# Capped attention feeding a two-layer MLP on one core: last key chunk in array quarters, row sums of a pair of head pairs in 112 columns, constants filled by GpSimd

## The chip, the cores and the metric

The kernel runs on one core of a Trainium2 chip. The number compared is the device time of the whole program in microseconds (us): the median of three runs of the kernel before was 580.81 us (580.37 to 581.53). The profile shown here is of one further execution, which took 580.01 us.

## The reference, cut to what matters

```python
# q, k, v: (4 batches, 12 heads, 448 tokens, 64); scale = 1/8; cap = 30
scores = scale * q @ k.T
scores = cap * tanh(scores / cap)
attn = exp(scores - max) / (sum(exp(scores - max)) + 1e-9)
x = (attn @ v)  -> heads side by side: (4 * 448, 768)
h = x @ w_in                                             # w_in: (768, 2048)
g = where(h >= 1, h, where(h <= -1, 0, (h + 1)**2 / 4))
out = g @ w_out                                          # w_out: (2048, 768)
```

## The kernel before, in words

**Names.** Two heads that share a batch make a head pair; there are 6 pairs in a batch and 24 in all, n = 0 to 23, and `d = n // 2` counts pairs of head pairs. S is 448 queries, P is 128, D is 64, HS is 224. The 448 keys are cut in chunks c = 0, 1, 2 of 128 keys and c = 3 of 64 keys. PSUM has eight banks: two tiles `s` of two banks each for scores, `f0` and `f1` for the MLP's products, one bank `av` for attention times values, one bank `t` for the row sums and for their reciprocals spread over partitions.

**Attention of one pair n** (`attention`). `split` cuts the loaded q and k into two fp16 parts. `qk` multiplies them in three products on 64x64 quarters of TensorE's array, four matmuls at a time. `expo` runs tanh and exp on ScalarE and writes fp32 tiles `e`. `av` multiplies values by `e`; the two heads of the pair use the left and the right 64 columns of the array, two matmuls at a time. For the last chunk, which has 64 keys, the two heads lie in the two halves of the partitions crosswise, and the values have blocks of zeros so that a full 128-row matmul picks the right half (`last_av`, 224 columns). Pairs 12 to 17 (`HALVED`) use fp16 parts of `e` and of the values, three products each, the others fp32.

**Row sums.** `add` adds chunks of `e` on VectorE as far as `direct(n)` says, and `norm` sums over partitions with matmuls of a matrix of ones, four at a time in 32 columns of the array each, 224 columns of data: for n < 6 three groups of four fp32 matmuls (the added chunks 0 and 1, then chunk 2, then chunk 3), for n = 6 to 11 two groups, from n = 12 on one. Both n of one d add into bank `t`. `divide` takes a reciprocal of (128, 224), cuts it in three bf16 parts stacked over rows (`low`), spreads it over partitions with two matmuls per n of 224 columns (`sel`), and scales the copy `xf` of the bank `av`.

**MLP.** fp16 parts again, three products of 448 columns (`across`, in `h_mm`, `o_mm`, `product`). A matmul of 128 columns of weights is issued either whole or as two of 64 columns side by side; `Plan.narrow` picks the second where the neighbours in TensorE's order are attention matmuls of that shape. Batches 2 and 3 are computed with seven products for eight, at the end.

**Order.** `ORDER` is a table that lists every step and its engine; the program is issued in exactly that order on each engine, and TensorE works in order. Where `either` gives several engines, the table picks one. The MLP's matmuls of batch 0 begin once the attention of batch 0 is divided; from then on they stand between the attention steps of later batches.

Of the kernel before, what the change touches and what calls it, by code (L numbers as in the profile page):

```python
# [14 lines left out]
BF16 = mybir.dt.bfloat16  # L15
# [11 lines left out]
VC = 2 * NCK + 2  # L27
# [48 lines left out]
HS = S // 2  # L76

# [9 lines left out]
    "c-mEW1E5^V^L15qb#-@a+qP}nwr$(CZQITw#%{P9+uV)0`DX5&m*4-JyqCGRQ8;z#bU%Pt5E}&IfPuJxpdcQEgZK~u2m}*ALWl^7ATcBXhDeYUEF^;{kQ`D#N(c{;!9gmB2B{$pq=gbt64F6gC<PTE"  # L87
    "Jw%5L5CbwoOvnTcp&XQk%uorcK^ABPS;1g7C=a!uHhhE@5EUvzbtnVbp)pw0kOL|}Rj30Fb3zr!1vQ`vgu|9l6T)Lts0(c&H?)EXm<$_0Gspu&p+2;OyzmKzK|bgRouEB5hkEcC+CYBz0-d1%%z<xE"
    "5L&|+7z@Lp5PXFgI2T61NGJ@+u^SYD@6ZE^!Z^r+9bhU<gi$aJy1;lS1}ShJOoHOj6S~86NQsMKJ}iJ<5EFaDWEc$--~gn?70?H!z!HdsePJc^gQai~X22R42!o(MbcF%15N5++m<5YqImE_Quof=D"
    "@30zvfpt&_2g5SB1ZglX4uOqu1kS*(Z~`_%DqIhTARZotvk(VoLIu1GCt(Y0f>ZDZ9D{4{7yJfo@Hm`?t*{NU;&#{p*>D5wgg+rW?t$yD7ygD`cmsC9Zn%oq@IDmAD{vd`z<Kx&>fudz0C(Xb+`t@I"  # L90
    "1dHMYcmh}9C7y$uI1O*XJ$QxBU?1GZJNO)O;v;wgFQFK|g8P^YZ{chB2Oi@Ctcd#|B0j;lPznFR;&>gO!ae*K-oYDqi0|PkR>ps^3RcAra2H?WTP%U~u>nTHcUTQ0;}3{}QL!O@#Iy)_1*733M2tk~"
    "kgzdE$F|rGN8n?Kk8dzNenN#A@ENwp1o#4*;8)Cu9Wfyuz>=5<8B1X!e2<aoGj_nzxCs+u8SI3;@eB6Bk=Pe=V;&rZ$tWs4$0WD}zhPedfur#QX2MgL6u)CW%#ZysIYptd7>#1kI7Es`nXv#8jlqIA"
    "0OL?~EQ>X;DK^7?7?*&e({wCOikN1gCZVO6fKpOTtc9^@CdQ)L7>~+fc{G%YX5lg{LCvuR&c@}KhFW4cT7myzXY7J=un*P2gj5$d<3QYkD=|C`!mgNzGEjVKg<CN#b;H5f9WAZGB-8_k;6Y4H8EG4~"
    "#_>1-58+VEM2GQLbhI6N;#^EhgJ~kp!(o_$($Nl_gumf0cp4{T7CM8&@htYG`M4Sv;6hx3e_%<Pg0*QX_M<;>5w69ZxDL<ZdhAb`X&3&EyKxR3!3~&|7UKZggNvyY4WW&A6o=9<8cxS>FAk(Zv=2+u"
    "T&hFqDI1lg<Cud+P(?bABWXX*qZ3$;%1~meOG{`JEu{!FpDIyRDo+=%GF`-Kw2UHBF3L%la5Rmfu{4gx(*&AGlV~zcp{X>D_Rs>VLM!Mb=BDYioEB0Zsz-|`FIAxWw3qTxb!tdWX(b(|%ead2(`s5n"
    "Yw0h{PU~nN{f+zS7g|pnXd`W+8PteoQUNMR2Wd0?O25$-Izor&D9xf{REW0HaoR?w)fGBG4d?`2rE9cK6{g#?otn`}x=z2-DLPGOXb0`2o79rdsI&A3{YmHOJYArRbca6CCAv&^=?3kh8dQX8QZ2ei"
    "x2QR_qV?(rZC0P@3pJq!bf0F^SBj$=(>L0p9#U)iPHm_K?NFfhsYmpfp3qa;png%mDpaKQtH0<!imQ~`skW-N#44UTr{b$k>KQ$!7xa>}I-p+BYdWj`p~R{v6(dnbS>;qX6<$S95mh7=Sw&G%)xY$H"
    "-coydN9R=sdQTlGq3T4PsS71i8`Um#NVTK?R1%d`T~NE}14UEORRWbvrBEr=HuX2fP%%|1m0JC&y3$vbMx|Bd_=noAs_<oXP^DApRS!C>x>0iVn_A4f18vij{!$rKMwLnJQJK{VbzOC*KU6IBx4NPB"
# [1340 lines left out]
```

## Time and profile before

| what | value |
|---|---|
| median of three runs | 580.81 us |
| the profiled execution | 580.01 us |
| its span (first to last instruction) | 578.1 us |
| TensorE busy | 568.7 us, 98% |
| VectorE busy | 517.8 us, 90% |
| ScalarE busy | 420.6 us, 73% |
| GpSimd busy | 1.3 us |

Busy is the time in which at least one instruction of an engine was under way. Matmuls overlap each other, so that a gap shorter than a matmul's own length does not show as idle time. The span leaves out 1.9 us at the program's ends.

### The profile page before, as it was taken

The page shows a single profiled execution, that of the slowest core. Times are in us where ns is not written, and L with a number is a line of the kernel's source. Part 1 is how long each engine was busy: PE and PEld are TensorE (multiplying, and loading weights), DVE is VectorE, ACT ScalarE, POOL GpSimd, SP SyncE. Part 2 cuts the span into 40 slices and gives each one's busy share as a digit, 9 for nine tenths or more (in the row PEclk, how much of TensorE's full clock was granted, in tenths as well). Part 3 has the DMA queues.
Part 4 walks back from the last instruction along what each step waited for, and adds up shares of the span by engine and source line. Part 5 has one row for each costly group of instructions (what it writes and reads, how often), then busy time and mean ns, then how long its engine had stood idle before and what let it go on. Part 6 is the DMA issues. An engine that isn't in the chain of part 4 may idle for free.

```text
span 578.1 us, 13988 instructions
## 1 busy us (share of the span) xinstructions
PE 568.7 (98%) x5685; PEld 319.1 (55%) x5685; DVE 517.8 (90%) x1017; ACT 420.6 (73%) x703; POOL 1.3 (0%) x6
## 2 busy tenths in 40 slices
PE   7999999999999999999999999999999999999997
PEld 3444554545454555556654545566666666666675
DVE  7999999999999999999998865899899999998712
ACT  6999998968558579989999897557877786541200
POOL 0000000000000000000000000000000000000000
PEclk9999999999999999999999999999999999999999
DMA  8879581767878412311789999994566656653202
GB/s 302 306 249 352 177 299 77 282 241 249 317 252 274 183 56 88 104 56 57 227 271 290 337 307 325 308 292 142 158 225 201 207 185 211 200 176 123 88 33 83
DMA packets 57000, 120.11 MB, mean 208 GB/s; under 512 B 4962, under 2 KB 35426, under 8 KB 55394
## 3 DMA queue, kind: packets, MB, share of 16 engines
q1 hardware_dynamic: 56784, 119.07, 61.1%
q8 instruction: 45, 0.74, 0.5%
q14 instruction: 25, 0.20, 0.1%
q10 hardware_dynamic: 146, 0.10, 0.1%
HBM read 91.42 MB, written 27.72 MB: 206 GB/s over the span
## 4 chain that ended last, share of the span: by engine, by line
PE 53%; DVE 4%; ACT 1%; issue 0%; DVEq 0%; ACTq 0%
PE f L268 24%; PE s L268 12%; PE av L268 7%; PE t L268 4%; PE av L483 2%; PE s L407 2%; PE av L388 1%; PE t L504 1%; DVE wr L611 1%; DVE g L545 0%; DVE z L425 0%; PE av L470 0%; DVE sums L452 0%; DVE sums L444 0%; PE s L403 0%
## 5 line engine op out<-in xcount | busy, mean ns | idle before, releaser
L268 PEld LDWEIGHTS <-w 128*64 128x64 f16 (+1 forms) x2997 | 206.8, 107 | 145.7 <-issue 5.3
L268 PE MATMUL f<-x,w 128*64 128x448 f16 (+1 forms) x939 | 122.8, 353 | 0.4 <-DVE wr L611 0.3
L268 PE MATMUL f<-g,w 128*128 128x448 f16 (+1 forms) x774 | 121.7, 353 | 0.0
L415 ACT ACTIVATE e<-s,tsc 128x896 f32<-128x896 f32 (+1 forms) x96 | 84.9, 910 | 16.6 <-PE s L407 9.4
L416 ACT ACTIVATE e<-e,capb 128x896 f32<-128x896 f32 (+1 forms) x96 | 89.6, 948 | 0.5
L407 PE MATMUL s<-spl 64*64 64x448 f16 x864 | 51.3, 357 | 2.2 <-ACT e L415 1.8
L483 PE MATMUL av<-e,vt 128*64 128x448 f32 x216 | 45.6, 549 | 0.2 <-ACT e L416 0.2
L610 ACT ACTIVATE r<-r 128x448 f32<-128x448 f32 x64 | 36.4, 573 | 1.0
L407 PEld LDWEIGHTS <-spl 64*64 64x64 f16 x864 | 21.9, 107 | 27.3 <-issue 17.5
L296 DVE SCALAR_TENSOR_TENSOR w<-z,w 128x768 f16<-128x768 f32 (+1 forms) x28 | 29.8, 1068 | 0.6 <-ACT w L295 0.5
L609 ACT ACTIVATE r<-f,half 128x448 f32<-128x448 f32 x36 | 22.5, 626 | 8.5 <-PE f L268 8.4
L444 DVE TENSOR_TENSOR sums<-e,e 128x896 f32<-128x896 f32 x24 | 26.1, 1088 | 0.7 <-ACT e L416 0.6
L365 DVE SCALAR_TENSOR_TENSOR spl<-qkr,spl 128x896 f16<-128x896 f32 (+2 forms) x25 | 26.2, 1048 | 0.5 <-ACT spl L377 0.2
L483 PEld LDWEIGHTS av<-e,vt 128*64 128x64 f32 x216 | 13.7, 136 | 22.0 <-issue 17.0
L319 ACT ACTIVATE z<-z 128x512 f32<-128x512 f32 x24 | 16.4, 685 | 10.9 <-DVE z L318 10.9
L545 DVE SCALAR_TENSOR_TENSOR g<-wr,g 128x448 f16<-128x448 f32 x37 | 22.8, 620 | 0.1
L268 PEld LDWEIGHTS <-spl 128*64 128x64 f16 x288 | 16.8, 110 | 10.4
L268 PEld LDWEIGHTS <-qkr 128*64 128x64 f16 x288 | 16.8, 110 | 10.4
L292 DVE SCALAR_TENSOR_TENSOR z<-w,z 128x768 int32<-128x768 int32 (+1 forms) x21 | 22.0, 1047 | 0.3
L291 DVE SCALAR_TENSOR_TENSOR z<-w,z 128x768 int32<-128x768 int32 (+1 forms) x21 | 22.0, 1046 | 0.3
L295 ACT ACTIVATE w<-z 128x768 f16<-128x768 f32 (+1 forms) x22 | 20.6, 942 | 1.2 <-DVE z L292 1.2
L611 DVE SCALAR_TENSOR_TENSOR wr<-f,r 128x448 f32<-128x448 f32 x33 | 20.4, 620 | 0.6 <-ACT r L610 0.4
(288 smaller groups left out, 947.9 us busy)
## 6 DMA issues: line engine op xcount, KB each, us to landing
w<-w_in SPq DMA_DIRECT2D x32, 384.0 KB, 5.4
z<-w_out SPq DMA_DIRECT2D x24, 512.0 KB, 5.6
w<-w_in SPq DMA_DIRECT2D x14, 768.0 KB, 7.7
qkr<-qkp SPq DMA_DIRECT2D x23, 448.0 KB, 5.0
vt<-vp SPq DMA_DIRECT2D x24, 320.0 KB, 4.9
w<-w_out SPq DMA_DIRECT2D x7, 1024.0 KB, 5.8
zd<-z SPq DMA_DIRECT2D x16, 384.0 KB, 3.2
zd<-z SPq DMA_DIRECT2D x12, 512.0 KB, 3.6
```

Of the source, the lines that this page charges most:

```text
L268: T.matmul(t[at:at + w], lhsT=lhs[:, at:at + w], rhs=rhs, start=start, stop=stop, skip_group_check=True)
L296: dve(width, lambda: V.scalar_tensor_tensor(out=parts[1], in0=zv, scalar=-WS, in1=parts[0], op0=ALU.mult, op1=ALU.subtract), zk + keys[0], ...
L365: dve(m, lambda: V.scalar_tensor_tensor(out=out, in0=full, scalar=scale, in1=high, op0=ALU.mult, op1=ALU.subtract, accum_out=fin[:, j:j + ...
L407: T.matmul(s[rows, j, :S], lhsT=t[own, a, at:at + D], rhs=t[own, b, :S], start=(i == 0), stop=(i == 2), tile_position=(own.start, rows.start))
L415: act(w * S + 60, lambda: A.activation(e[:, :w] if c < 3 else e[:, 0].rearrange("p (h s) -> p h s", h=2), s[:, :w, :S] if c < 3 else s[:, ...
L416: act(w * S + 111, lambda: A.activation(e[:, :w], e[:, :w], AF.Exp, scale=capb), ek + [("tsc", None)], ek)
L444: dve(2 * S, lambda: V.tensor_tensor(out=t, in0=e0, in1=e, op=ALU.add), ek0 + ek, tk)
L483: T.matmul(a[h, :S], lhsT=vt[:, j * 3 + c], rhs=e[:, j], start=(c == 0), stop=(c == 2), skip_group_check=True)
L545: dve(S, lambda: V.scalar_tensor_tensor(out=t[:, 1], in0=full, scalar=scale, in1=t[:, 0], op0=ALU.mult, op1=ALU.subtract), r + hk, lk)
L609: act(S + (170 if acc else 60), lambda: A.activation(r, src, AF.Relu, bias=half, scale=0.5 * root / (WS * XS), **acc), key + [("half", Non ...
L610: act(S, lambda: A.activation(r, r, AF.Square, scale=math.sqrt(WS * XS / GS)), rk, rk)
L611: dve(S, lambda: V.scalar_tensor_tensor(out=w, in0=src, scalar=WS * XS, in1=r, op0=ALU.max, op1=ALU.min), key + rk, wk)
```

## The change

- **Last chunk in quarters.** The scores of chunk 3 are written so that head j lies in column block j and the query halves lie in the two halves of the partitions. `last_av` then uses 64x64 quarters of the array, four matmuls at a time, two banks `av0` and `av1` for the two query halves. The values lose their zero blocks (VC from 10 to 8 blocks of 64 columns).
- **Chunks 0 to 2** are written to the two banks in two halves of 224 columns (`full_av`), and copied out in two halves by ScalarE or VectorE (`norm`).
- **Sums of a d in 112 columns.** For each n the four query quarters stand in four rows of the ones (`ones[:, 2 * g + u]`), so that the sums of both n of a d fill 112 columns in place of 224 (`sums_of`). `direct` is 1 for n < 6: all four chunks go to TensorE. From n = 6 on it is 4: all chunks are added on VectorE and TensorE sums once per n.
- **Reciprocal and its parts** are 112 columns wide (`total`); the spread takes four matmuls of 112 columns per n in place of two of 224 (`divide`).
- **Banks.** Bank `t` is gone (its place is `av1`). The sums and the spreads use `f0` and `f1` for n < 6 and the score tiles `s0` and `s1` afterwards. For n of 6 and more, `total` and `divide` stand inside the attention of the next pair.
- **Constants** (`ones`, `halves`, `sel`, `low`) are filled by GpSimd, 111 fills, in place of 54 on VectorE.
- **ORDER** is a new table.

```diff
-VC = 2 * NCK + 2
+VC = 2 * NCK
...
-    "c-mEW1E5^V^L15qb#-@a+qP}nwr$(CZQITw#%{P9+uV)0`DX5&m*4-JyqCGRQ8;z#bU%Pt5E}&IfPuJxpdcQEgZK~u2m}*ALWl^7ATcBXhDeYUEF^;{kQ`D#N(c{;!9gmB2B{$pq=gbt64F6gC<PTE"
+    "c-n1ObD$nqu%DSTXU;jXZ5wTD+cujf4I10FZQC~5xJernabw$V-?zKp?R$T`z4yD{?ws-bX67z{074`%&>seX1%l*|0#bs5RFE3dKx7yQF(EBPfpm}_VnI|G0wZ7$M1u^F5u!sTNCKH53uJ|CkR5VB"
...
-    fs, avs, ts = [bank("f%d" % i) for i in range(2)], [bank("av0")], [bank("t0")]
+    fs, avs = [bank("f%d" % i) for i in range(2)], [bank("av%d" % i) for i in range(2)]
...
-            T.matmul(a[own, cols], lhsT=v[:, VC - 4 + 2 * half + j], rhs=e[:, cols], start=False, stop=stop, skip_group_check=True)
+            T.matmul(avs[half][own, :HS], lhsT=v[rows, VC - 2 + j], rhs=e[rows, block], start=False, stop=stop, tile_position=(rows.start, own.start), skip_group_check=True)
+
+    def full_av(c, v, e, start, stop):
+
+        for half in range(2):
+            for j in range(2):
+                T.matmul(avs[half][j * D:(j + 1) * D, :HS], lhsT=v[:, j * 3 + c], rhs=e[:, j, half * HS:(half + 1) * HS], start=start, stop=stop, skip_group_check=True)
...
-        return 2 if n < NPR else 3 if n < PAIRED else NCK
+        return 1 if n < NPR else NCK
...
-        act(S - 67, lambda: A.copy(xf, a[:, :S]), ak, fk)
...
+        for half in range(2):
+            part = slice(half * HS, (half + 1) * HS)
+            either([avk[half]], [(fk[0][0], half)], ("ACT", 262, lambda half=half, part=part: A.copy(xf[:, part], avs[half][:, :HS])), ("DVE", 300, lambda half=half, part=part: V.tensor_copy(xf[:, part], avs[half][:, :HS])))
...
+    def room_t(n):
+        if n < NPR:
+            return take("f", fs)
+        t, k = take("s", ss)
+        return t[:, 0], k
...
+                        T.matmul(t[q:q + 32, :QS4], lhsT=w, rhs=m, start=(begin + i == u == 0), stop=(begin + i == whole - 1 and u == 1), tile_position=(0, q), skip_group_check=True)
...
-        dve(1467, lambda: V.reciprocal(rr, t[:, :S // 2]), tk, rk)
+        dve(690, lambda: V.reciprocal(rr, t[:, :QS4]), tk, rk)
...
+                for k in range(4):
+                    across(t[:, k * QS4:(k + 1) * QS4], sel[:, 2 * g + k % 2, k // 2], mix[:, 1], k == 0, k == 3)
...
+    fill = lambda t, value, key: pool(100 + t.free_size() // 2, lambda: G.memset(t, value), [], [(key, None)])
```

**TensorE, attention of n = 0.** These are the values' products of the first pair's last two chunks and its row sums; `e2` and `e3` are exp of chunks 2 and 3, `av0` the output. Before:

```order
L483 MATMUL av0_147<-e2_102,vt0_98 64x448 x2
L388 MATMUL av0_147<-e3_103,vt0_98 64x224 x4
```

and its sums, a few rows on:

```order
L504 MATMUL t0_148<-sums0_108,ones_77 32x224 x4
L504 MATMUL t0_148<-e2_102,ones_77 32x224 x4
L504 MATMUL t0_148<-e3_103,halves_78 32x224 x4
```

The same two places now:

```order
L397 MATMUL av0_147<-e2_102,vt0_98 64x224 x2
L397 MATMUL av1_148<-e2_102,vt0_98 64x224 x2
```

```order
L528 MATMUL f0_145<-e2_102,ones_77 32x112 x8
L528 MATMUL f0_145<-e3_103,halves_78 32x112 x8
L391 MATMUL av0_147<-e3_103,vt0_98 64x224 x2
L391 MATMUL av1_148<-e3_103,vt0_98 64x224 x2
```

The last chunk keeps four matmuls of 224 columns, now in quarters of the array (L391); a full chunk has four of 224 in place of two of 448 (L397); sums of one chunk are eight matmuls of 112 columns in place of four of 224, go to `f0`, and read `e` directly where VectorE's `sums0` stood.

**TensorE, row sums of n = 6 and 7 (d = 3).** Before, one run of sums in bank `t0`:

```order
L504 MATMUL t0_148<-sums0_108,ones_77 32x224 x4
L504 MATMUL t0_148<-e2_102,halves_78 32x224 x4
L504 MATMUL t0_148<-sums1_109,ones_77 32x224 x4
L504 MATMUL t0_148<-e1_101,halves_78 32x224 x4
L483 MATMUL av0_147<-e3_103,vt1_99 64x448 x2
```

Now, in a score tile, between two products of the MLP:

```order
L271 LDWEIGHTS w1_84
L271 MATMUL f1_146<-x5_115,w1_84 128x448
L528 MATMUL s0_143<-sums0_108,ones_77 32x112 x8
L528 MATMUL s0_143<-sums1_109,ones_77 32x112 x8
L271 LDWEIGHTS w1_84
L271 MATMUL f0_145<-x0_110,w1_84 128x448
```

The sums stand in `s0`, so that the next scores in `s0` follow the reciprocal; the last chunk's matmuls (`halves`) are gone and its add is VectorE's.

**ScalarE, batch 0.** Rows around the copy of the second pair's `av` (`xf1`); L377 and L380 are the first half of `split`, L506 and L499 the copy of `av`. Before:

```order
L415 ACTIVATE e0_100<-s0_143,tsc_75 128x896
L506 COPY xf1_138<-av0_147 128x448
L416 ACTIVATE e1_101<-e1_101,capb_73 128x448
L415 ACTIVATE e2_102<-s0_143,tsc_75 128x896
L416 ACTIVATE e0_100<-e0_100,capb_73 128x896
L377 ACTIVATE spl0_96<-qkr0_94 128x896
L415 ACTIVATE e3_103<-s1_144,tsc_75 128x896
```

Now:

```order
L424 ACTIVATE e2_102<-s0_143,tsc_75 128x896
L499 COPY xf1_138<-av1_148 128x224
L499 COPY xf1_138<-av0_147 128x224
L425 ACTIVATE e1_101<-e1_101,capb_73 128x448
L425 ACTIVATE e0_100<-e0_100,capb_73 128x896
L425 ACTIVATE e2_102<-e2_102,capb_73 128x896
L424 ACTIVATE e3_103<-s1_144,tsc_75 128x896
```

The copy is in two halves, and the split of the next pair (L377) is not on ScalarE here any more; it stands on VectorE.

## Rows read from the trace of the kernel before

**Rows 1.** The page: busy time by engine, then the last chain's share.

```profile
PE 568.7 (98%) x5685; PEld 319.1 (55%) x5685; DVE 517.8 (90%) x1017; ACT 420.6 (73%) x703; POOL 1.3 (0%) x6
...
PE 53%; DVE 4%; ACT 1%; issue 0%; DVEq 0%; ACTq 0%
```

**Rows 2.** ScalarE, batch 0, in order of time: start us, us, instruction.

```profile
7.81 1.91 ACT L415 ACTIVATE e<-s,tsc 128x896 f32<-128x896 f32 x2 [1.42 <-PE s L407]
...
29.77 0.96 ACT L377 ACTIVATE spl<-qkr 128x896 f16<-128x896 f32 x1
30.61 1.92 ACT L415 ACTIVATE e<-s,tsc 128x896 f32<-128x896 f32 x2
...
42.81 0.55 ACT L506 COPY xf<-av 128x448 f32<-128x448 f32 x1
43.22 1.64 ACT L416 ACTIVATE e<-e,capb 128x896 f32<-128x896 f32 x2
44.73 0.40 ACT L517 CAST mix<-rest 128x224 bf16<-128x224 f32 x1
45.00 1.94 ACT L415 ACTIVATE e<-s,tsc 128x896 f32<-128x896 f32 x2
...
58.76 1.51 ACT L415 ACTIVATE e<-s,tsc 128x448 f32<-128x448 f32 x2
```

**Rows 3.** TensorE at the end of batch 0's attention, in order of time.

```profile
60.42 1.33 PE L407 MATMUL s<-spl 64*64 64x448 f16 x24
```

**Rows 4.** Stretches: busy us (instructions) of PE, PEld, DVE, ACT, POOL; clock, DMA.

```profile
7.81:60.27 52.46, 49.04 (x624) 22.35 (x616) 50.15 (x99) 51.54 (x67) 0.00 (x0) 1.00 0.84 302
60.42:573.00 512.58, 512.23 (x5023) 293.55 (x5024) 461.46 (x874) 365.72 (x633) 0.68 (x1) 1.00 0.60 200
...
60.00:264.00 204.00, 203.68 (x1867) 107.84 (x1866) 200.71 (x299) 162.52 (x237) 0.00 (x0) 1.00 0.54 189
```

**Rows 5.** The chain that ended last, in order of time: start us, us, what.

```profile
264.03 3.60 PE f L268 x36
...
278.96 0.57 PE av L388 x12
...
291.49 0.19 PE t L268 x4
291.69 2.25 PE av L483 x12
293.94 0.76 PE av L388 x8
294.70 0.69 PE s L407 x12
295.39 0.29 PE s L403 x12
...
305.80 6.92 PE f L268 x36
...
360.41 0.89 PE t L504 x16
...
389.82 3.40 PE f L268 x36
```

**Rows 6.** Groups by line and shape, VectorE.

```profile
L444 DVE TENSOR_TENSOR sums<-e,e 128x896 f32<-128x896 f32 x24 | 26.1, 1088 | 0.7 <-ACT e L416 0.6
...
L514 DVE RECIPROCAL rr<-t 128x224 f32<-128x224 f32 x12 | 18.6, 1553 | 0.1
```

**Rows 7.** GpSimd's start in order of time, then the instructions on `low`.

```profile
0.33 0.10 POOL L1425 MEMSET const-uint8-127<- 128x1 uint8 x1
0.79 0.47 POOL L653 MEMSET x<- 128x448 f16 x1 [0.36 <-POOLq L1425]
...
L686 DVE MEMSET low<- x32: 59/59/59, 2.2 to 28.7; 6x1 f32 x8, 3x1 f32 x8, 4x1 f32 x4, 1x1 f32 x4
L518 DVE SCALAR_TENSOR_TENSOR rest<-mix,low,rr x12: 444/450/461, 29.8 to 370.1; 128x224 f32<-128x224 bf16 x12
```

More of the change, by code (lines that the diff above doesn't have):

```diff
@@ L198, in fast_body @@
     capb, capr, tsc, half = new("capb", [P, 1]), new("capr", [1, 1]), new("tsc", [P, 1]), new("half", [P, 1])
[L199 to L200 removed]
+    ones, halves = new("ones", [P, 4, 32]), new("halves", [P, 4, 2, 32])
+    sel, low = new("sel", [P, 4, 2, P], BF16), new("low", [P, 2])
     fin = new("fin", [P, NFIN])
@@ L478, in run @@
                 if c == 3:
[L479 removed]
+                    last_av(vt, e[:, 0], True)
                     continue
[L481 to L484 removed]
+                full_av(c, vt, e, c == 0, c == 2)
+        kind = ("r" if cs[0] == 3 else "a") + ("r" if cs[-1] == 3 else "a")
+        pe(sum(762 if c < 3 else 378 + 95 * (len(cs) > 1) for c in cs), run, [k for c in cs for k in st["e", n, c][1]] + vk + (avk if cs[0] else []), avk, kind)
     def sums_at():
@@ L490, in norm @@
     def norm(n):
-        (sm, mk), (a, ak), g = st["sums", n], st["av", n], n % 2
-        if g == 0:
-            st["t", n // 2] = take("t", ts)
-        t, tk = st["t", n // 2]
         xf, fk = st["xf", n] = take("xf", xfs)
-        late = range(direct(n), NCK)
-        def run():
-            for c in [None, *late]:
-                for j, q, half in sums_at():
-                    m = sm if c is None else st["e", n, c][0]
-                    w, m = (ones[:, g], m[:, j, half]) if c != 3 else (halves[:, g, (j + (half.start > 0)) % 2], m[:, 0, half])
-                    T.matmul(t[q:q + 32, :S // 2], lhsT=w, rhs=m, start=(g == 0 and c is None), stop=(g == 1 and c == (late[-1] if late else None)), tile_position=(0, q))
@@ L505, in norm @@
-        pe(402 + 385 * len(late), run, mk + [k for c in late for k in st["e", n, c][1]] + [("ones", None), ("halves", None)] + (tk if g else []), tk, "tt")
-        act(S - 67, lambda: A.copy(xf, a[:, :S]), ak, fk)
-        if g:
-            divide(n // 2)
-    def divide(d):
+        for half in range(2):
+            part = slice(half * HS, (half + 1) * HS)
+            either([avk[half]], [(fk[0][0], half)], ("ACT", 262, lambda half=half, part=part: A.copy(xf[:, part], avs[half][:, :HS])), ("DVE", 300, lambda half=half, part=part: V.tensor_copy(xf[:, part], avs[half][:, :HS])))
@@ new lines, in norm, with sums_of @@
+        if n % 2:
+            waiting.append(n // 2)
+            if n < NPR:
+                settle()
+    def room_t(n):
+        if n < NPR:
+            return take("f", fs)
+        t, k = take("s", ss)
+        return t[:, 0], k
+    def sums_of(d, runs):
+        if ("t", d) not in st:
+            st["t", d] = room_t(2 * d)
+            turn["t", d] = 0
+        t, tk = st["t", d]
+        begin, turn["t", d] = turn["t", d], turn["t", d] + len(runs)
+        whole = sum(NCK - direct(2 * d + g) + 1 for g in range(2))
+        def run():
+            for i, (g, c) in enumerate(runs):
+                for u in range(2):
+                    for j, q, half in sums_at():
+                        n, z = 2 * d + g, int(half.start > 0)
+                        m = st["sums", n][0] if c is None else st["e", n, c][0]
+                        at = half.start + u * QS4 if c != 3 else j * HS + u * QS4
+                        w, m = (ones[:, 2 * g + u], m[:, j, at:at + QS4]) if c != 3 else (halves[:, 2 * g + u, z], m[:, 0, at:at + QS4])
+                        T.matmul(t[q:q + 32, :QS4], lhsT=w, rhs=m, start=(begin + i == u == 0), stop=(begin + i == whole - 1 and u == 1), tile_position=(0, q), skip_group_check=True)
+        pe(17 + 385 * len(runs), run, [k for g, c in runs for k in (st["sums", 2 * d + g][1] if c is None else st["e", 2 * d + g, c][1])] + [("ones", None), ("halves", None)] + (tk if begin else []), tk, "tt")
@@ L516, in divide @@
         for q, (src, sk, out, ok) in enumerate(((rr, rk, rest, ek), (rest, ek, mix[:, 1], ml))):
-            either(sk, mh, act_(S // 2, lambda src=src: A.copy(mix[:, 0], src)), dve_(S // 2, lambda src=src: V.tensor_copy(mix[:, 0], src), True))
-            dve(S // 2 + 58, lambda q=q, src=src, out=out: V.scalar_tensor_tensor(out=out, in0=mix[:, 0], scalar=low[:, q:q + 1], in1=src, op0=ALU.mult, op1=ALU.add), sk + mh + [("sel", None)], ok)
+            either(sk, mh, act_(QS4, lambda src=src: A.copy(mix[:, 0], src)), dve_(QS4, lambda src=src: V.tensor_copy(mix[:, 0], src), True))
@@ L519, in divide @@
+            dve(QS4 + 58, lambda q=q, src=src, out=out: V.scalar_tensor_tensor(out=out, in0=mix[:, 0], scalar=low[:, q:q + 1], in1=src, op0=ALU.mult, op1=ALU.add), sk + mh + [("sel", None)], ok)
         if 2 * d in HALVED:
@@ L537, in divide, with settle @@
                 halves_of(x, xk, xf, 1.0, fk, FX + n - (HC if n >= 3 * NPR else 0))
+    def settle():
+        while waiting:
+            total(waiting[0])
+            divide(waiting.pop(0))
     def halves_of(t, key, full, scale, r, j=None):
@@ L576, in attention @@
                 qk(n, [c, c + 1])
+            if waiting and c == 1:
+                total(waiting[0])
             expo(n, c)
+            if waiting and c == 3:
+                divide(waiting.pop(0))
             add(n, c)
+            if n < NPR and c % 2:
+                sums_of(n // 2, [(n % 2, c - 1), (n % 2, c)])
             if n in HALVED:
```

198 lines of the change are left out of this document (102 added, 96 removed).

## The prediction

> **What bounds the kernel now.** I read the page first. TensorE is busy 98% of the span, and the chain that ended last is almost all TensorE's where it is anybody's [rows 1]; in order of time it is TensorE alone from 264.03 us to the last copies [rows 5]. So a microsecond of TensorE's stream taken away is a microsecond gained, provided that TensorE then finds its data ready. I next read busy time by stretch, because a share over the whole span hides stages. From 60.42 us on TensorE is busy 512.23 of 512.58 us. Before that, from 7.81 us (the first tanh) to 60.27 us, it is ScalarE that has no pause, 51.54 of 52.46 us, and TensorE has some, 49.04 us [rows 4]. So there are two stages: batch 0's attention at the pace of ScalarE, and then TensorE. VectorE is not far off in either: 50.15 of 52.46 us, and 200.71 of 204 between 60 and 264 us [rows 4].
>
> **TensorE's stream, part by part.** The chain in order of time prices each kind of matmul from its start to the start of the next kind [rows 5].
>
> *Last chunk, fp32 (18 head pairs).* The row at 293.94 us has x8 in 0.76 us: four matmuls of 224 columns, each of two instructions, two side by side. Four side by side should take half, 0.38 us. That fp16 quarters of the array do run four at a time is the row of L403: x12 in 0.29 us, where L388's fp16 form, two at a time, needs 0.57 for the same x12. That fp32 may run four at a time, in 32-column strips, is the row of L504 at 360.41: x16 in 0.89. So 18 x 0.38 = **6.8 us less**. The bounds are 0 (if fp32 quarters run two at a time) and 6.8; I take 6.8, to which both rows point.
>
> *Last chunk, fp16 (6 pairs).* 0.57 becomes 0.29: 6 x 0.28 = **1.7 less**.
>
> *Chunks 0 to 2 in halves.* Now 2.25 us for three fp32 chunks (291.69), 0.75 each; four matmuls of 224 columns are exactly the row at 293.94, 0.76. 54 chunks: **0.3 more**, with what fp16 adds.
>
> *Row sums.* A group is four concurrent fp32 matmuls of 224 columns, or now eight of 112. I counted the groups: 18 + 12 + 6 x 2 = 42 before, 24 + 6 + 12 = 42 now. Equal columns, so **0**. The bound below is nothing; the bound above would be the fixed cost of twice the instructions. L403's row has a weight load and a matmul each 24 ns (0.29 us over 12), and the sums would need no faster rate (16 in 0.38 us), so I keep 0.
>
> *Spreads.* Two matmuls of 224 bf16 columns per pair become four of 112. The row at 291.49 us gives 0.19 for one pair. Bounds: 0.19 again, or 0.38 if a matmul of 112 columns takes as long as one of 224 (24 x 0.19 = 4.6 more). In the 11 pairs where the spread uses 64-column tiles the rate needed is again L403's, so 0; the 13 pairs with whole 128-column weights need one load of 128 columns each 47 ns, which no row shows, and I take the middle, 13 x 0.095 = **1.2 more**.
>
> The Trainium skill (TensorE: Matmul & The Clock Gate, Back-to-back issue gap) gives about 81 ns per load and matmul of 128 columns in a sustained stream. No run here has shown it; L403's 24 ns shows that it cannot hold for tiles. By it the 52 whole spread matmuls would take 34 ns more each than 112 columns need, 1.8 us where I have 1.2, and the sum would be 0.6 us higher.
>
> *Changes of array shape.* L407's x12 at 294.70 comes after 64-column tiles and takes 0.69, against 0.57 for three groups of four at 448 columns (twice 0.29, from L403, which follows L407 without a change of shape). So a change costs about 0.12; I use 0.11. Counted over TensorE's orders there are 117 such changes before and 132 now, since quarters now stand behind the full chunks and the sums stand in more places: 15 x 0.11 = **1.7 more**.
>
> *Weights whole or halved.* After the last attention the MLP's products go from two of 64 columns to one of 128. 18 narrow products took 3.40 us (389.82, x36), 36 whole ones 6.92 with one change of shape (305.80): 0.189 each both times. **0.**
>
> TensorE together: -6.8 - 1.7 + 0.3 + 1.2 + 1.7 = **-5.3 us**.
>
> **Batch 0, at ScalarE's pace.** The scores of the eighth head pair begin at 60.42 us [rows 3], when ScalarE ends the tanh that starts at 58.76 (1.51 for two) [rows 2]. I compared ScalarE's order up to this tanh in both programs. Tanh and exp are the same 54. Gone to VectorE are three splits (0.84 each, from 29.77 to 30.61), one weight cast of 768 columns (0.72, scaled from that split by columns) and one cast of x (0.41, priced like the copy at 42.81, whose successor starts at 43.22). Five copies of 0.41 become ten halves (estimate 0.22 each, +0.1), and one cast `mix` of 0.27 (44.73 to 45.00) becomes five of half the width (estimate 0.18 each, +0.6). Sum -2.5 - 0.7 - 0.4 + 0.1 + 0.6 = -2.9. TensorE itself has 1.4 us less to do up to the same scores: 18 MLP products (3.4) come later, two chunks of the seventh pair (1.5) and three changes of shape (0.3) come earlier, six last chunks (-2.3) and six more groups of sums (+2.3) cancel, halves add 0.2. So TensorE's idle time here shrinks by 2.9 - 1.4 = **1.5 us**; the 1.4 is in the sum above already.
>
> VectorE must take what ScalarE gives away. It loses in this stage six adds (1.09 each [rows 6], L444), most of the constants, and half of each reciprocal (L514, 1.55 for 224 columns, estimate 0.8 for 112); it gains splits and copies. It gets lighter, by some 8 us up to 264 us, although six pairs get an add of the last chunk that TensorE summed.
>
> **The banks.** The sums and spreads of nine d stand in the score tiles, three uses each. On TensorE whatever is queued behind waits too. In the order at d = 3, 18 MLP products (3.4 us) stand between the sums in `s0` and the next scores, enough for a reciprocal of 0.8 us; a d like it costs nothing. For VectorE's lateness now and then I take **0.5 us**.
>
> **The sum.** -5.3 - 1.5 + 0.5 = -6.3 us. Against the profiled execution (span 578.1, time 580.01) that is 571.8 and 573.7; the median of the runs is 0.8 above it, so that I predict 580.8 - 6.3 = **574.5 us**.
>
> **Rivals.**
>
> *Score tiles are late (other side).* `total` and `divide` wait for tanh to free a tile, and the next scores wait for VectorE to read it. VectorE at 98% between 60 and 264 us [rows 4] speaks for it; the MLP products in between speak against it. It decides from 6.8 / 9 = 0.75 us per d on. At 1 us per d it costs 9: 580.8 - 6.8 + 9 = 583. With half of that price the result is 578.5.
>
> *GpSimd's fills are late.* VectorE reads `low` first at 29.8 us (L518) and filled it until 28.7 [rows 7]. GpSimd now has 111 fills in a row. At 0.10 each (the constant at 0.33, which is the nearest row for small fills) with 1.1 for the large `sel` (estimate, 1024 elements, from 0.47 for 448 at 0.79) and 1.3 before them (GpSimd's busy time, [rows 1]) it ends near 13.5 us; if each took the 0.47 of that wide fill it would end near 54, batch 0 would stand still until then for at least 15 us, and the time be about 595. From (29.8 - 2.4) / 111 = 0.25 us per fill on it costs. The Trainium skill (SBUF — State Buffer, Who interferes with whom) says that GpSimd and VectorE lock each other out of a shared port while VectorE runs its double-rate copies and scalings. In the trace GpSimd does nothing beside VectorE, so nothing here shows it; the few such VectorE instructions of the first 15 us hold back some 4 us in all and leave the fills in time.
>
> *VectorE sets the pace to 264 us.* Then its 8 us less are worth as much there, TensorE's late savings (about 3) come on top, and the time is near 570. That TensorE has no idle time there speaks against it.
>
> *fp32 quarters run two at a time.* The change doesn't do what it says: -6.3 + 6.8, 581.3. L403 and L504 speak against it.
>
> **How the numbers follow.** Forecast (572.5 to 577): 0.62. VectorE's pace, 569 to 572.5: 0.13. Late score tiles: 0.17, of which 0.07 still end under 579.6, 0.05 within 0.2% and 0.05 above. Late fills 0.04, slower. Two at a time 0.04, mostly no change. About 0.2% (1.2 us) is what a measurement of this kernel can tell from no change. So faster 0.82, same 0.08, slower 0.10. The range 570.3 to 580.5 takes in the spread's bounds (-1.2, +3.4) and the half-price case of late score tiles; it leaves out about 0.05 below and 0.13 above.
>
> **What the profile after would show.** The chain in order of time: the last chunk's row (L391) x8 near 0.38 plus a change of shape, fp16 x12 near 0.29; the full chunks x24 in 2.3; sums of a d in 0.38 per group. If L391 shows 0.76 the fourth rival is right. GpSimd's last fill should start before 15 us, and ScalarE reach the scores of the eighth pair near 57.5 us with TensorE's idle time before it smaller. TensorE busy near 562 us. Waits of TensorE's scores or sums for a reciprocal or for the scaling of `xf`, more than 0.5 us per d, would make the prediction wrong; so would spreads of 0.38 us each.

## The result and the profile after

The changed kernel took 570.83 us (median; 569.58 to 571.32) beside 580.59 for the kernel before, a ratio of 0.9826 with a 95% interval of 0.9806 to 0.9847. It is 9.8 us faster where 6.3 were forecast. The profiled execution took 570.54 us with a span of 568.7, 9.4 less than before.

The page of the changed kernel: busy time by engine, and the last chain's share.

```profile
PE 560.5 (99%) x5590; PEld 316.2 (56%) x5590; DVE 504.6 (89%) x974; ACT 411.6 (72%) x710; POOL 12.9 (2%) x117
...
PE 97%; ACT 2%; DVE 0%; issue 0%; POOL 0%; POOLq 0%; DVEq 0%
```

TensorE lost 8.2 us of busy time [rows 1], and more than that is gone from the span, so that idle time went too. The same stretches as in [rows 4], from the first tanh to the scores of the eighth pair, and from there on:

```profile
7.55:57.10 49.55, 47.24 (x952) 30.61 (x944) 46.74 (x86) 49.28 (x71) 6.72 (x71) 1.00 0.88 319
57.23:563.00 505.77, 505.77 (x4604) 282.13 (x4603) 452.65 (x876) 360.41 (x637) 0.49 (x1) 1.00 0.59 198
57.23:264.00 206.77, 206.77 (x2447) 121.32 (x2449) 204.14 (x314) 173.86 (x262) 0.00 (x0) 1.00 0.53 185
```

Batch 0 ends 3.2 us earlier (57.23 for 60.42 us); ScalarE is still without a pause in it. From 57.23 us on TensorE has no idle time at all, and VectorE is at 99% as far as 264 us. The chain in order of time, in batch 0 and at three later places, shows the new forms:

```profile
50.50 0.90 PE f L528 x32
51.40 2.42 PE av L397 x24
53.82 0.54 PE av L391 x8
...
233.19 0.90 PE s L528 x32
...
236.49 0.41 PE av L391 x12
...
241.27 0.39 PE s L271 x8
...
305.29 0.76 PE av L397 x8
306.04 0.54 PE av L391 x8
306.58 0.57 PE s L416 x12
```

L391 x8 is the last chunk in fp32: 0.54 us, of which four at a time is 0.38 and the rest belongs to the change of array shape ahead of it; x12 in fp16 takes 0.41 on the same terms. [Rows 5] have 0.76 and 0.57 without a change. The 32 sums of 112 columns take 0.90 where 16 of 224 took 0.89. The spreads (L271 on `s`, x8) take 0.39 for both n of a d with whole weights, 0.19 to 0.20 for each n, as before.

### The profile page after: what moved, and what is told of

It reads as the page before. It is cut to its first block, busy times and chain, and to the rows that moved or that the text cites. A ratio compares the mean times of both kernels' runs of the same rounds, so it can differ in the third digit from the quotient of the medians.

```text
span 568.7 us, 13886 instructions
## 1 busy us (share of the span) xinstructions
PE 560.5 (99%) x5590; PEld 316.2 (56%) x5590; DVE 504.6 (89%) x974; ACT 411.6 (72%) x710; POOL 12.9 (2%) x117
## 4 chain that ended last, share of the span: by engine, by line
PE 97%; ACT 2%; DVE 0%; issue 0%; POOL 0%; POOLq 0%; DVEq 0%
PE f L271 50%; PE s L271 13%; PE av L271 11%; PE av L397 9%; PE s L416 7%; PE av L391 2%; PE f L528 2%; PE s L528 1%; PE s L412 1%; ACT e L424 1%; PE f L699 1%; ACT e L425 1%; DVE wr L854 0%; PE av L702 0%; POOL x L693 0%
## 5 line engine op out<-in xcount | busy, mean ns | idle before, releaser
L271 PEld LDWEIGHTS <-w 128*128 128x128 f16 (+1 forms) x2460 | 188.6, 103 | 162.0 <-issue 9.6
L271 PE MATMUL f<-x,w 128*64 128x448 f16 (+1 forms) x978 | 124.4, 353 | 0.0
L271 PE MATMUL f<-g,w 128*64 128x448 f16 (+1 forms) x840 | 124.3, 353 | 0.0
L397 PE MATMUL av<-e,vt 128*64 128x224 f32 x432 | 46.5, 355 | 0.0
L397 PEld LDWEIGHTS av<-e,vt 128*64 128x64 f32 x432 | 29.6, 137 | 11.7 <-issue 2.1
L416 PEld LDWEIGHTS <-spl 64*64 64x64 f16 x864 | 23.4, 107 | 21.7 <-issue 10.9
L298 ACT ACTIVATE w<-z 128x1024 f16<-128x1024 f32 (+1 forms) x21 | 20.0, 951 | 10.0 <-DVE z L295 10.0
L462 DVE TENSOR_TENSOR sums<-sums,e 64x448 f32<-64x448 f32 x36 | 22.2, 617 | 0.8
L322 ACT ACTIVATE w<-w 128x384 f32<-128x384 f32 x32 | 18.0, 564 | 5.2 <-DVE w L321 5.2
L271 PEld LDWEIGHTS <-qkr 128*128 128x128 f16 x144 | 14.1, 98 | 13.1
```

Source lines behind the costliest of these rows:

```text
L271: T.matmul(t[at:at + w], lhsT=lhs[:, at:at + w], rhs=rhs, start=start, stop=stop, skip_group_check=True)
L322: act(width + 155, lambda: A.activation(hi.bitcast(F32), hi.bitcast(F32), AF.Relu, accum_out=chp[:, i, part:part + 1]), zk, zk + [("chp", ...
L397: T.matmul(avs[half][j * D:(j + 1) * D, :HS], lhsT=v[:, j * 3 + c], rhs=e[:, j, half * HS:(half + 1) * HS], start=start, stop=stop, skip_g ...
L416: T.matmul(s[rows, j, :S], lhsT=t[own, a, at:at + D], rhs=t[own, b, :S], start=(i == 0), stop=(i == 2), tile_position=(own.start, rows.start))
L462: dve(S, lambda rows=rows, half=half: V.tensor_tensor(out=tq[rows, :, half], in0=tq[rows, :, half], in1=eq[rows], op=ALU.add), ek + tk, tk)
```

## The experiments

Each kernel was timed beside the kernel before; a difference to the changed kernel below is that of the two ratios, times 580 us, and such a figure is good to about 1.5 us, since both ratios have their interval. To see where in the program a difference arises, I read from TensorE's timeline when the scores of head pair n begin (n counts from 0, so that 7 is the eighth pair), in the experiment less in the changed kernel (the last column is the last matmul; us):

```
n              1     3     5     7     8    12    18   last
one: halves  -0.2   0.6   1.7   2.2   2.9   4.1   5.2   7.4
two: splits  -1.1  -0.3   0.9   1.2   2.8   2.8   2.8   2.8
four          0.1   0.1   0.6   0.7   1.0   2.3   3.5   5.4
five: x4      0.1   0.1   0.1   0.1   0.1   7.7  11.6  20.8
nine: x2     -0.1  -0.1  -0.1  -0.1  -0.1   2.2   2.5   4.7
ten           0.1   0.1   0.5   0.5   0.5   0.6   0.6   0.6
eleven        0.3   0.4   0.4   0.3   0.3   3.9   6.2  11.0
```

**One: the last chunk without quarters.**

```diff
-T.matmul(..., lhsT=v[rows, VC - 2 + j], rhs=e[rows, block], ..., tile_position=(rows.start, own.start), ...)
+T.matmul(..., lhsT=v[:, VC - 2 + j], rhs=e[:, block], ...)
```

> The changed kernel, but the last chunk's values are multiplied over all 128 rows of the array, two matmuls at a time instead of four in quarters; the same matmuls of 224 columns in the same order, with other weights and data (the output then holds the other half's keys too). Theory A (the quarters are the gain, and TensorE is the bound): after batch 0, 12 pairs at 0.38 and 6 at 0.28 us more, less 5 changes of shape at 0.095, is 5.7; batch 0's 6 pairs add 2.3 and 3 changes of shape, of which the idle time there hides a part: 576.5 to 579.4 us, 1.2% to 0.2% under the kernel before. Rival B (the gain came from ScalarE, VectorE and the fills, and TensorE finds slack for this): 570 to 572 us.

Measured: 0.9965 (0.9952 to 0.9979), 8.1 us more than the changed kernel, as theory A has it (576.5 us, its lower end, is 0.6 to 0.7% under the kernel before, not 1.2%). The chain at the place that the last three rows above show:

```profile
311.43 0.76 PE av L397 x8
312.18 0.76 PE av L391 x8
312.94 0.69 PE s L416 x12
```

Three rows take 2.21 us where the changed kernel needs 1.87. The change of shape has only moved, from ahead of the last chunk to behind it (0.69 for 0.57). The table says that the pairs of batch 0 count in full too: 2.2 us by n = 7, against 2.3 for six pairs and 0.3 for changes of shape.

**Two: three splits back on ScalarE.**

```diff
-V.tensor_scalar(t[:, 0, w], raw[:, w], scalar1=QS, ...)
+A.activation(t[:, 0, w], raw[:, w], AF.Copy, scale=QS)   # n in (2, 4, 5)
```

> The changed kernel, but three splits of q and k in batch 0 (n = 2, 4, 5) are ScalarE's, at the places in the program where VectorE had them. Theory A (ScalarE sets the pace of batch 0): three times 0.84 us on ScalarE, 572.4 to 573.4 us where the changed kernel has 570.8. Rival B (TensorE or VectorE sets the pace there): VectorE is rid of three times 0.54 us, 569.5 to 571 us.

Measured: 0.9876 (0.9861 to 0.9891), 2.9 us more: theory A. The 2.5 us on ScalarE come out in full, within the noise, although VectorE is lighter by 1.6. (The profiled execution was 1.1 us ahead at n = 1, and 2.8 behind from n = 8 on.) Together with the first experiment this says that batch 0 is a chain through two engines. A microsecond more on either shows.

**Three: VectorE fills the constants.**

```diff
-pool(100 + t.free_size() // 2, lambda: G.memset(t, value), [], [(key, None)])
+pool(100 + t.free_size() // 2, lambda: V.memset(t, value), [], [(key, None)])
```

> The changed kernel, but VectorE fills the constants, at the same places in the program. 111 fills of about 0.06 us are 6.6 us on VectorE in the first 16 us. Theory A (VectorE sat idle for over 5 us of the first 10, and takes most of the fills there): 571 to 573 us. Rival B (batch 0 stands behind VectorE from its start): all of it shows, 576 to 578 us. Rival C (GpSimd's fills disturb VectorE by more than they relieve it): under 570 us.

Measured: 0.9971 (0.996 to 0.9981), 8.4 us more, above even rival B. VectorE's idle time in the first 10 us was no room: 2.7 us of it is the wait for the first load, and nearly all fills stand behind that wait in VectorE's order, ahead of work that is urgent. VectorE's timeline of this kernel:

```profile
3.93 0.53 DVE L380 TENSOR_SCALAR spl<-qkr 128x704 f16<-128x704 f32 x1 [2.73 <-DMA qkr<-qkp]
...
8.85 0.11 DVE L707 MEMSET sel<- 3x64 bf16 x1
8.97 0.15 DVE L720 TENSOR_SCALAR tsc<-tsc 128x1 f32<-128x1 f32 x1
```

`tsc`, for which the first tanh waits, is written at 8.97 us, in the changed kernel at 5.85. TensorE's next scores wait for that tanh to free their tile, and the stretches of this kernel show what that cost besides:

```profile
9.00:10.00 1.00, 0.00 (x0) 0.00 (x0) 0.66 (x8) 0.78 (x1) 0.00 (x0) 1.00 1.08 380
...
12.00:13.00 1.00, 0.00 (x0) 0.00 (x0) 0.94 (x5) 1.00 (x3) 0.00 (x0) 0.50 0.21 82
13.00:14.00 1.00, 0.99 (x12) 0.57 (x15) 0.93 (x4) 1.00 (x2) 0.00 (x0) 0.50 0.00 0
...
17.00:18.00 1.00, 1.00 (x10) 0.69 (x8) 0.96 (x2) 0.72 (x1) 0.00 (x0) 0.50 0.94 387
```

After TensorE stood idle from 9 to 10 us and worked only in part to 12, the granted clock is 0.50, the level of 1.2 GHz, until 18 us. The changed kernel stands idle for a like time and keeps 1.00:

```profile
10.00:11.00 1.00, 0.00 (x0) 0.00 (x0) 0.97 (x2) 1.00 (x2) 0.73 (x10) 1.00 1.04 409
```

How the 8.4 us divide between the late scores and the lower clock is not shown.

**Four: all products and spreads with whole weights.**

```diff
-if "a" in (kind(k - 1)[1], kind(z)[0]):
+if False:
```

> The changed kernel, but every product of the MLP and every spread is issued with whole weights of 128 columns, none as two of 64. Changes of array shape rise from 134 to 174 over the program, 2 of the 40 in batch 0. Theory A (a change costs 0.095 us whatever stands there): 38 x 0.095 = 3.6 us, 574.4 us. Rival B (half as many matmuls and weight loads give back what the changes cost): 570 to 571.5 us.

Measured: 0.9932 (0.9918 to 0.9945), 6.1 us more; the last matmul of the profiled execution starts 5.4 us later. Above theory A, and rival B is out. 0.7 of the 5.4 us have arisen by n = 7, in batch 0, which has only 2 of the 40 changes; what costs them is not shown. The other 4.7 over 38 changes is 0.12 us each, close to the 0.11 of the prediction.

**Five and nine: the reciprocal four times and twice, from d = 3 on.** The diff is that of five; nine has 2 in place of 4.

```diff
-V.reciprocal(rr, t[:, :QS4])
+[V.reciprocal(rr, t[:, :QS4]) for _ in range(1 if 2 * d < NPR else 4)]
```

> The changed kernel, but from d = 3 on VectorE takes each reciprocal four times over (the same result), 0.85 us each, so that it leaves the score tile 2.6 us later in nine d. In the trace of the changed kernel the next scores in that tile start 2.2 us (d = 3), 2.9, 4.2, 0.8, 1.7, 3.1, 3.7 and 0.3 us after the reciprocal. Theory A (score tiles were no cost here but stand close to it): waits of 0.4, 1.8, 0.9 and 2.3 us appear, and with VectorE's lateness 575 to 580 us. Rival B (the tiles were a cost already): every d adds all 2.6, 594 us. Rival C (TensorE never meets them): 570 to 571.5 us.

> The changed kernel, but from d = 3 on VectorE takes each reciprocal twice (the same result), 0.85 us more in nine d. With four times (2.55 us more) nearly all showed: 21.7 us of 23. Theory A (VectorE has no room left, or the wait for the reciprocal is on the path at every d): 6 to 7.7 us more than the changed kernel, ratio to the kernel before near 0.994. Rival B (there is room of some 0.8 us per d, which the larger step used up): 0 to 2 us more, ratio 0.9825 to 0.986.

Measured: four times 1.0195 (1.0177 to 1.0214), 21.4 us more; twice 0.9925 (0.9907 to 0.9943), 5.7 us more. Theory A of five fell: it counted the time in which a score tile stood unused, which is not VectorE's room. Rival B has nearly the size, 21.4 of 23, but the tile is only a part of it. Nine is just under theory A's range and far from rival B. TensorE's waits from 57 to 400 us, with four (us in total, times, longest):

```profile
PE s L412 <- DVE rr L538: 4.6, 4, 1.9
PE f L271 <- DVE wr L651: 4.0, 3, 1.9
PE s L271 <- ACT e L424: 3.8, 2, 2.0
PE s L271 <- DVE mix L542: 2.4, 2, 2.2
```

The first row is the score tile, and the third is the same tile from the other side: a spread waits for the tanh that still reads the tile (at one of its two places `mix` was ready only 0.3 us earlier). The second and fourth are work that stood behind the reciprocal on VectorE (the gate's `wr`) or waited for it (`mix`). With two, the rows are:

```profile
PE f L271 <- DVE wr L651: 1.3, 2, 0.7
PE s L271 <- DVE mix L542: 0.4, 1, 0.4
PE f L271 <- DVE w L299: 0.3, 1, 0.3
PE s L271 <- ACT e L424: 0.2, 1, 0.2
```

They are 2.2 of the 4.7 us; the rest hides under matmuls. Comparing the starts of the same matmuls in both kernels, I can place 4.4 us: 2.7 at products that wait for `wr` or `w`, 0.8 for `mix`, 0.9 for a score tile. So VectorE has next to no room: 0.85 us per d costs 0.5 to 0.6. This also says what the halved reciprocal is worth in the changed program: with one about as long as before (twice 0.85 for 1.55 us) 5.7 of the 9.8 us gained are lost again.

**Seven: relief for ScalarE and VectorE in batch 0**, in two kernels: the high parts of the splits of n = 2 to 7 on GpSimd, and, in the first of them, the copies of `av` and the casts `mix` on VectorE too.

```diff
-V.tensor_scalar(t[:, 0, w], raw[:, w], ...)
+(G if 2 <= n < 8 else V).tensor_scalar(t[:, 0, w], raw[:, w], ...)
...
-A.copy(xf[:, part], avs[half][:, :HS])
+(V.tensor_copy if n < NPR else A.copy)(xf[:, part], avs[half][:, :HS])
...
-A.copy(mix[:, 0], src)
+(V.tensor_copy if 2 * d < NPR else A.copy)(mix[:, 0], src)
```

> The changed kernel, but in batch 0 GpSimd makes the high parts of the splits of n = 2 to 7 (VectorE loses 6 x 0.54 us), and VectorE takes the copies of av and the casts mix that ScalarE had (ScalarE loses about 3.1 us, VectorE gains 3.8). Theory A (ScalarE sets the pace of batch 0, and TensorE follows): TensorE fell behind its own stream by 1.8 us between 20 and 57 us, so 569 to 570 us where the changed kernel has 570.8. Rival B (VectorE or the longer path through GpSimd sets the pace): 571 to 574 us.

> The changed kernel, but in batch 0 GpSimd makes the high parts of the splits of n = 2 to 7, and VectorE is rid of 6 x 0.54 us; ScalarE as it was. Theory A (ScalarE sets the pace): 570.3 to 571.3 us, no change. Rival B (VectorE sets it): 567.5 to 569.5 us. Rival C (GpSimd takes so long that scores come late, or holds VectorE up): over 572 us.

Measured: 1.0089 (1.0074 to 1.0105) and 1.0022 (1.0011 to 1.0033), 15 and 11 us more than the changed kernel; the first is outside both of its theories, the second is rival C. In the second kernel, GpSimd's group, its timeline, and TensorE's scores of n = 2:

```profile
L380 POOL TENSOR_SCALAR spl<-qkr 128x896 f16<-128x896 f32 x6 | 16.8, 2808 | 26.6 <-PE s L412 17.1 <-issue 9.4
```

```profile
22.07 2.49 POOL L380 TENSOR_SCALAR spl<-qkr 128x896 f16<-128x896 f32 x1 [9.37 <-issue]
24.61 0.27 POOL L707 MEMSET low<- 1x1 f32 x3
...
29.87 0.42 POOL L707 MEMSET low<- 3x1 f32 x4
```

```profile
24.61 0.59 PE L416 MATMUL s<-spl 64*64 64x448 f16 x4 [6.56 <-POOL spl L380]
```

A split takes 2.8 us here, 0.62 on VectorE, and the fills of `low` behind the first end at 30 us for 16. But the slow split is not the main part of the loss. The first split begins at 22.07 us, 4 us after TensorE's last work (it ends at 18.1 us); GpSimd had been idle since 12.7, from 20.1 us on no engine works at all, and the profile names no reason (in the first kernel the first split begins at 23.06 us, also 4 us after TensorE's last work). TensorE waits 6.56 us for it, and its granted clock is 0.50 from 23 to 29 us. The second kernel is 0.9 us ahead of the changed one at n = 1, 5.8 behind at n = 2, 10.1 at n = 4 and 11.0 at the end: the last three splits, no shorter than the first, cost 0.9 us together. Whether ScalarE's relief alone would have paid is not told by this.

**Eight: the kernel before, with its 54 fills on GpSimd.**

```diff
-dve(..., lambda: V.memset(...), ...)
+dve(..., lambda: G.memset(...), ...)
```

> The kernel before, but GpSimd fills the 54 constants at the same places in the program, and VectorE is rid of 54 x 0.06 us in the first 29 us. Theory A (ScalarE sets the pace of batch 0 before too): 580 to 580.8 us, no change beyond 0.2%. Rival B (VectorE stood behind its fills): up to 3.2 us less, 577.5 to 579.5 us.

Measured: 0.9981 (0.997 to 0.9992), 1.1 us less than before, between 0.5 and 1.7. Rival B, at a third of its length. VectorE counts in batch 0 as well, in some places.

**Ten: without the last chunk's adds on VectorE.**

```diff
-V.tensor_tensor(out=tq[rows, :, half], in0=tq[rows, :, half], in1=eq[rows], op=ALU.add)
+V.tensor_tensor(out=tq[rows, :, half, :2], in0=tq[rows, :, half, :2], in1=eq[rows, :, :2], op=ALU.add)
```

> The changed kernel, but VectorE adds only two columns of the last chunk into the row sums in each of the 36 adds of line 462 (the sums then lack nearly all of that chunk); VectorE is rid of about 36 x 0.45 us, 11 us of it before 264 us. Theory A (TensorE sets the pace, VectorE only stands close to it): ratio to the kernel before 0.9815 to 0.983, as the changed kernel. Rival B (VectorE sets the pace up to 264 us): 3 us or more less, ratio under 0.978.

Measured: 0.9837 (0.9822 to 0.9852), the changed kernel's time within the noise (0.6 us more). Theory A: taking work from VectorE gains nothing, while (nine) giving it some costs at once. The two engines are level up to 264 us.

**Eleven: the spreads four times over, from n = 6 on.**

```diff
-for k in range(4):
+for k in list(range(4)) * (1 if n < NPR else 4):
```

> The changed kernel, but from n = 6 on the four spread matmuls (eight where halved) are issued four times over (the same values are written each time), which leaves all else as it was. Theory A (a spread of 112 columns costs by its columns, 0.196 us per n, as the rows of the changed kernel say): 18 x 3 x 0.196 = 10.6 us more, ratio to the kernel before 1.001. Rival B (whole weights of 128 columns cost 0.095 us per n more, as the prediction took): 10 n of the 18 are whole, 13.4 us more, ratio 1.006.

Measured: 1.0023 (1.0013 to 1.0034), 11.4 us more. The table separates the theories better: the difference rises by 1.18 us at each of the nine d, 10.6 in all, and by as much where weights are whole as where they are halved. That is theory A, 1.18 / 6 = 0.197 us per n. TensorE's timeline of a d with halved weights in the changed kernel, then in this one:

```profile
90.78 0.56 PE L271 MATMUL s<-mix,sel 128*64 128x112 bf16 x16
```

```profile
91.12 1.74 PE L271 MATMUL s<-mix,sel 128*64 128x112 bf16 x64
```

**Twelve: the kernel before, with light adds.** The figures of 5.0 and 3.6 us in its expectation are TensorE's time from matmul to matmul after batch 0, less their columns at the rates of [rows 5] and 0.095 us for each change of shape. They hang on how these rates are rounded: with 0.189 us for 448 columns everywhere they are 4.7 and 3.8.

```diff
-V.tensor_tensor(out=t, in0=t, in1=e, op=ALU.add)
+V.tensor_tensor(out=t[:, :, :2], in0=t[:, :, :2], in1=e[:, :, :2], op=ALU.add)
...
-V.tensor_tensor(out=tq[rows, at], in0=tq[rows, at], in1=eq[rows, of], op=ALU.add)
+V.tensor_tensor(out=tq[rows, at, :2], in0=tq[rows, at, :2], in1=eq[rows, of, :2], op=ALU.add)
```

> The kernel before, but from n = 6 on VectorE adds only two columns (per head or quarter) of chunks 2 and 3 into the row sums, in lines 447 and 452 (the sums then lack nearly all of these chunks); VectorE is rid of some 18 x 1.0 and 36 x 0.3 us. After batch 0 TensorE of the kernel before lost 5.0 us against its own stream, that of the changed kernel 3.6. Theory A (the difference is TensorE's wait for VectorE's adds and for what stands behind them): 1.0 to 1.5 us less, ratio 0.9975 to 0.9983. Rival B (it is the groups' own cost on TensorE, not a wait): ratio 0.9995 to 1.0005.

Measured: 0.997 (0.9958 to 0.9981), 1.7 us less than before; in the profiled executions the last matmul starts 1.4 us earlier, all of it gained at three places, between 234 and 252, 251 and 269, and 299 and 313 us, and the loss of 5.0 us falls to 3.5. TensorE's timeline shows the first place, in the kernel before and in this one:

```profile
244.96 1.38 PE L504 MATMUL t<-sums,ones 128*32 128x224 f32 x16
```

```profile
245.01 0.96 PE L504 MATMUL t<-sums,ones 128*32 128x224 f32 x16
```

The sums waited for the last chunk's adds, which VectorE did between other work; so at the third place. At the second, 0.5 us at 262 and 264 us, it is products that waited for the gate's `wr`, which stood behind the adds. Theory A.

## Why the prediction was right, and where it was 3.5 us short

The direction and the bound were right; the sum was too small by 3.5 us. 570.83 us lies in the range, but only 0.5 above its lower end, and outside the 572.5 to 577 us that had most of the chance: the terms that were off were all off to the same side. Step by step:

- **Last chunk in quarters, -8.5.** Right: taking the quarters away costs 8.1 us by the runs, 7.4 in the profile (one).
- **Halves, sums and weights, about 0.** Right by the rows above (0.76 for a chunk, 0.90 for 32 sums).
- **Changes of array shape, +1.7.** Right in kind: 0.11 us each lies between the 0.095 of four's expectation and the 0.12 of its profile.
- **Spreads, +1.2: mis-sized.** The cost is 0. Whole weights of 128 columns with 112 columns of data run at the rate of the columns, 49 ns each; eleven shows no fixed cost. The back-to-back gap of about 81 ns that the Trainium skill gives (TensorE: Matmul & The Clock Gate, Back-to-back issue gap) does not hold here either.
- **Batch 0, its end 2.9 earlier.** The time was right: 57.23 us, 3.2 earlier. The mechanism was too simple. ScalarE does set the pace (two), but what TensorE has to do there counts as well (one, 2.2 us), and VectorE partly: the fills, which the prediction moved away at no gain, were worth about 1.1 us to the kernel before (eight). How the 3.2 us divide among the three is not settled, since their shares overlap.
- **Score-tile waits, +0.5: mis-sized.** The profile after has none: TensorE is busy without a pause from 57.23 us, and the count from start to start, in the next point, finds none under its matmuls either. But this rival was nearer than I thought: the point from which it decides was set at 0.75 us per d, and 0.85 us more on VectorE costs 0.5 to 0.6 us per d (nine), mostly through other work on VectorE and not through the tile.
- **TensorE's waits for VectorE after batch 0, taken as 0: the term that was missing.** [Rows 4] show TensorE busy 203.68 of 204 us, and I read that as no idle time. It hides waits shorter than a matmul's own length, among them the 0.4 us of the sums at 245 us, whose instructions overlap while they wait. Twelve shows 1.4 to 1.7 us of them that come from adds alone. Counted from start to start, by runs of matmuls of one kind, the kernel before has six places after batch 0 that take over 0.08 us more than their columns and changes of shape, 1.8 us together; the changed kernel has none, and lighter adds no longer gain anything there (ten). What TensorE loses after batch 0 falls by 1.4 us (5.0 to 3.6), or by 0.9 with the one rate (4.7 to 3.8); what is left comes in small amounts all over the stream.

With these terms put right, -6.3 - 1.2 - 0.5 - 0.3 - 1.4 is -9.7, or -9.2 with 0.9 for the last, against 9.4 in the spans and 9.8 in the medians. The parts can't be read as gains of their own: taking the quarters away (one), doubling the reciprocal (nine) and giving VectorE the fills (three) cost 8.1, 5.7 and 8.4 us, together far more than the 9.8 that the change gained.

Of the rivals, two at a time and late fills are out. GpSimd's fills took longer than forecast, the last at 16.1 us and not before 15, and no instruction waited for them. VectorE's pace, the rival from 569 to 572.5 us, has the measured time in its range, but only a small part of its mechanism: against the kernel before, VectorE's lightness was worth about 1.4 us after batch 0, not 8 up to 264 us. Late score tiles did not come, though doubling the reciprocal brings VectorE's lateness at once.

## What to carry to other kernels

Busy time of a pipelined engine is no proof that it never waits: compare its stream from start to start with what its rows say it needs, since waits shorter than an instruction hide under the instruction before. Where two engines are level, work taken from the one that stands second gains nothing and work given to it costs most of its length (here 0.5 to 0.8 us of 0.85); find out which with one kernel in each direction. Before moving small operations to another engine, look at what stands ahead of and behind them in its order: a queue that works in order has room only where they stand, not where it is idle.

## What the hardware showed that was not expected

**GpSimd and VectorE held each other up.** The timeline of the changed kernel between 12.1 and 13.5 us, GpSimd and then VectorE:

```profile
12.24 0.52 POOL L707 MEMSET sel<- 3x64 bf16 x1
12.33 0.78 POOL L707 MEMSET low<- 3x1 f32 x4
13.15 0.34 POOL L707 MEMSET sel<- 12x64 bf16 x2
```

```profile
12.11 0.56 DVE L297 TENSOR_SCALAR w<-z 128x768 f16<-128x768 f32 x1
12.70 0.96 DVE L299 SCALAR_TENSOR_TENSOR w<-z,w 128x768 f16<-128x768 f32 x1
```

The fill at 12.24 lasts until VectorE's TENSOR_SCALAR has ended and takes 0.52 us, while its like takes 0.14 when VectorE runs something else or nothing; after 3.5 us every fill over 0.4 us lies beside a TENSOR_SCALAR. With splits on GpSimd it is the other way round, in VectorE's timeline of the second kernel of seven:

```profile
26.59 1.17 DVE L297 TENSOR_SCALAR w<-z 128x768 f16<-128x768 f32 x1
...
34.71 0.94 DVE L541 CAST mix<-rest 128x112 bf16<-128x112 f32 x1
```

Both lie beside a split on GpSimd (26.01 to 28.87 and 34.33 to 37.10 us); in the changed kernel they take 0.56 and 0.22 us. The Trainium skill (SBUF — State Buffer, Who interferes with whom) says that the two engines share a pair of ports, that VectorE's double-rate forms of these operations need it, and that whoever comes second is held for the whole of the other's instruction. The fills agree with that. The second fence agrees that VectorE is held, but not that it is for the whole split: both operations end over a microsecond before it does.

**GpSimd is slow at the split.** 2.49 us for 128x896 from fp32 to fp16 at 22.07 us, when VectorE ran nothing beside it, against 0.62 on VectorE.
